# A fused attention and two-layer chain on one core: weight loads issued by ScalarE, a softmax moved to VectorE, weight combinations spread out

## The chip, the cores and the metric

One core of a Trainium2 chip runs the whole program in one launch. The metric is the device time of one execution in microseconds (us), the median of the runs shown. One further execution was profiled, and all rows below are of that one. A difference of about 0.2% (2.7 us) is what repeated runs of this kernel can tell from none.

## What is computed

Chunked attention (batch 8, 8 heads, 576 positions, chunks of 64, head size 64), then two feed-forward stages over the 4608 tokens of width 512:

```python
scores = scale * q_c @ k_c.T                 # per chunk of 64
attn = exp(scores - max) ; attn /= sum + 1e-9
x = (attn @ v_c) as [4608, 512]
h = x @ w_in                                 # [512, 2048]
x = (max(h, 0) + log1p(exp(-abs(h)))) @ w_out
h = max(max(x @ w1, x @ w2), x @ w3)         # [512, 768] each
out = h @ w_out2
```

The weights arrive as 64-bit floats and are turned into pairs of 32-bit parts on VectorE. Every product is done three times, on high and low parts (the table `PASS`), so TensorE runs 128x128 by 128x512 matrix multiplications nearly all the time.

## The kernel before

The 4608 tokens are nine blocks of 512. Blocks 0 to 2 go straight through the first feed-forward stage (`mlp1`). Blocks 3 to 8 go in three pairs by a scheme that saves one product in eight: seven products (`p1` to `p7` of `UnitA`) for each of eight **units** of a pair, where a unit is two columns of weights for both blocks. The weights of a unit are combinations made once (`weightsa`, during block 2), stored in DRAM as `wac` (three to a unit) and `wae` (one to two units), and loaded again for each pair by `againa`: 77 loads of 512 KB in all, each into one of six places named `ringa`. The last stage, `Triple`, works on three blocks at once with combinations `w2c` of its weights, made by `weights3` and stored in DRAM.

Every piece of work is an entry of a `Plan` (class `Plan`): the engines that may do it with a cost for each, what it reads and writes, what places it needs and a due time. `Plan.order` runs through a clock of its own, takes the entry with the earliest due time among those that are ready and whose places are free, and so writes down one fixed order for each engine. On the chip each engine then works through its list in order and waits at a row until what that row needs is there. So a row that waits holds up all rows behind it on its engine, data transfers that the engine issues among them.

Four things of this stage matter here:
- `againa` (L1034 to L1053) puts the loads of a unit's weights on GpSimd's queue, beside the loads of `v` (`loads`, L468), the stores of combinations (`w2c`, L926; `wso`, L1233) and the loads of the later weights (`conv`, L318).
- The attention tiles of blocks 5 to 8 are done between the units (`attention` with `apart=True`). Their `softmax` subtracts the maximum inside eight ScalarE activations, one for each 64 columns, which also accumulate the sums (L562).
- `keep` (L1134) copies a product of a unit out of the PSUM bank `ph`, which the next product into this bank needs back; `soft` (L1143) is the activation, and `cut_up` splits its result into high and low parts `g` for the second matrix. `finish` (L773) copies four accumulator banks `acc` out at the end of a block.
- `combos` (L1203) makes combinations of the second matrix for the last pair. The table `COMBOS` (L986) says behind which step of pair 0's second half each of its four calls stands.

## Time and profile before

| | |
|---|---|
| median of the runs (3 runs, lowest and highest) | 1368.36 us (1367.06, 1369.38) |
| the profiled execution, its own time | 1365.48 us |
| its span, first to last instruction | 1363.6 us |
| granted TensorE clock, mean over the span | 0.994 |
| TensorE busy with matrix multiplications | 1333.2 us, 98% |
| VectorE, ScalarE, GpSimd busy | 983.7, 545.0, 321.7 us |
| bytes moved | 289.38 MB, mean 212 GB/s |

Times in rows count from the first instruction of the span. Block 2 ends and pair 0 begins at about 340 us, pair 1 at about 517, pair 2 at about 679; the last stage begins near 830. Lines such as L1120 are those of the kernel before: L1120 is a product of a unit, L1419 the second matrix, L597 the small products of an attention tile, L281 a copy or cast on ScalarE, L288 a two-operand instruction on VectorE, L1156 the activation, L1045 a load of a unit's weights.

### The profile page before, as it was taken

How to read it: one execution, taken by the hardware profiler on the slowest of the kernel's cores; microseconds unless marked ns; L12 is line 12 of the kernel's file. 1: busy time of each engine (PE TensorE's matmuls, PEld its weight loads, DVE VectorE, ACT ScalarE, POOL GpSimd, SP SyncE). 2: the span in 40 equal slices, each digit the busy share in tenths (PEclk: the TensorE clock that was granted, in tenths of full speed). 3: DMA queues.
4: the chain of work that ended last, by engine and by line, in shares of the span. 5: the costliest groups of instructions: out<-in, count | busy, mean ns of one | idle time of the engine just before them, and what ended most of it. 6: DMA issues, size and time to landing. Idle time of an engine off the chain costs nothing.

```text
span 1363.6 us, 23089 instructions
## 1 busy us (share of the span) xinstructions
PE 1333.2 (98%) x8616; PEld 1094.0 (80%) x8616; DVE 983.7 (72%) x1527; ACT 545.0 (40%) x1199; POOL 321.7 (24%) x561
## 2 busy tenths in 40 slices
PE   5899999999999999999999999999999999999998
PEld 4788887888888887787788887888888888888887
DVE  8999965797576898657868898779714597145951
ACT  4544434464544645445535454432123222132211
POOL 2011555542233324323211122121111122011100
PEclk8999999999999999999999999999999999999999
DMA  8565567677689999978966789655644465344401
GB/s 254 159 201 154 134 181 201 189 273 228 169 257 258 267 302 301 280 252 297 366 209 237 259 311 338 234 192 193 219 162 144 155 231 206 141 148 154 139 25 68
DMA packets 218863, 289.38 MB, mean 212 GB/s; under 512 B 121601, under 2 KB 146625, under 8 KB 218753
## 3 DMA queue, kind: packets, MB, share of 16 engines
q0 software_dynamic: 53792, 178.26, 38.1%
q1 hardware_dynamic: 164144, 108.87, 26.9%
q8 instruction: 68, 1.11, 0.3%
q10 hardware_dynamic: 816, 0.79, 0.2%
q14 instruction: 43, 0.34, 0.1%
HBM read 196.61 MB, written 91.23 MB: 211 GB/s over the span
## 4 chain that ended last, share of the span: by engine, by line
PE 86%; DVE 5%; issue 4%; DMA 2%; POOL 1%; ACT 1%; SPq 0%; DVEq 0%; POOLq 0%; ACTq 0%
PE acc L1567 14%; PE both L1567 13%; PE acc L825 10%; PE ph L805 9%; PE ph L1120 8%; PE acc L1419 7%; PE one L1120 6%; PE both L1665 6%; PE acc L1665 5%; PE acc L1342 2%; PE ph L1342 2%; PE acc L1265 2%; DVE s L288 1%; PE aps L503 1%; POOL rv L468 1%
## 5 line engine op out<-in xcount | busy, mean ns | idle before, releaser
L288 DVE TENSOR_TENSOR s<-s,s 128x1024 f32<-128x1024 f32 (+3 forms) x222 | 213.8, 992 | 11.8 <-DMA x2d<-s 5.5
L1419 PE MATMUL acc<-g,s 128*128 128x512 f32 x768 | 184.5, 393 | 3.0 <-ACT tmp L281 2.2
L1419 PEld LDWEIGHTS acc<-g,s 128*128 128x128 f32 x768 | 142.6, 188 | 35.2 <-ACT tmp L281 3.1
L1120 PE MATMUL ph<-s,s 128*128 128x512 f32 x576 | 144.1, 389 | 1.4 <-DMA s<-wac 0.7
L805 PE MATMUL ph<-s,s 128*128 128x512 f32 x576 | 140.4, 394 | 0.0
L825 PE MATMUL acc<-g,s 128*128 128x512 f32 x576 | 139.8, 392 | 0.0
L1120 PEld LDWEIGHTS ph<-s,s 128*128 128x128 f32 x576 | 108.0, 188 | 24.6 <-DMA s<-wac 1.2
L805 PEld LDWEIGHTS ph<-s,s 128*128 128x128 f32 x576 | 108.3, 189 | 23.1
L825 PEld LDWEIGHTS acc<-g,s 128*128 128x128 f32 x576 | 107.3, 188 | 22.6
L281 ACT CAST s<-s 128x512 fp32r<-128x512 f32 (+1 forms) x106 | 86.3, 831 | 93.4 <-DVE s L1598 31.2
L1567 PE MATMUL acc<-s,s 128*128 128x512 f32 x452 | 120.3, 389 | 0.0
L1550 POOL DMA_DIRECT2D s<-w2c x105 | 56.0, 533 | 266.2 <-PE both L1567 87.5
L281 ACT CAST g<-s 128x1024 fp32r<-128x1024 f32 (+1 forms) x64 | 58.7, 919 | 144.6 <-PE both L1567 37.3
L1567 PE MATMUL acc<-g,s 128*128 128x512 f32 x400 | 110.0, 389 | 0.0
L1120 PE MATMUL one<-s,s 128*128 128x512 f32 x432 | 106.4, 390 | 0.9 <-ACT p L562 0.9
L1567 PE MATMUL both<-s,s 128*128 128x512 f32 x400 | 106.3, 389 | 0.0
L288 DVE TENSOR_TENSOR g<-tmp,g 128x512 fp32r<-128x512 f32 x104 | 70.6, 680 | 44.3 <-ACT g L281 44.2
L1567 PE MATMUL both<-g,s 128*128 128x512 f32 x368 | 100.1, 389 | 0.0
L1567 PEld LDWEIGHTS acc<-s,s 128*128 128x128 f32 x452 | 84.9, 188 | 17.6
L1120 PEld LDWEIGHTS one<-s,s 128*128 128x128 f32 x432 | 80.9, 188 | 18.5 <-ACT p L562 1.8
L468 POOL DMA_DIRECT2D rv<-in_v_dram x103 | 63.5, 620 | 104.5 <-issue 55.3
L1567 PEld LDWEIGHTS both<-s,s 128*128 128x128 f32 x400 | 75.1, 188 | 15.6
(158 smaller groups left out, 2159.5 us busy)
## 6 DMA issues: line engine op xcount, KB each, us to landing
s<-w2c POOLq DMA_DIRECT2D x105, 512.0 KB, 4.5
s<-wac POOLq DMA_DIRECT2D x66, 512.0 KB, 6.5
w2c<-s POOLq DMA_DIRECT2D x45, 512.0 KB, 5.2
wac<-s POOLq DMA_DIRECT2D x24, 512.0 KB, 5.1
s<-in_moe_w_dram POOLq DMA_DIRECT2D x18, 512.0 KB, 5.6
s<-x2d POOLq DMA_DIRECT2D x18, 512.0 KB, 5.8
s<-in_moe_w_in_dram SPq DMA_DIRECT2D x16, 512.0 KB, 6.2
s<-in_moe_w_out_dram SPq DMA_DIRECT2D x16, 512.0 KB, 5.7
```

What stands on the lines that cost most here:

```text
L281: nc.scalar.copy(dst(), src())
L288: return op({"D": 0.69 * n}, lambda e: nc.vector.tensor_tensor(dst(), a(), b(), f), r=r, w=w, **kw)
L468: dma(out=dst().rearrange("p (c e d) -> p c e d", e=2, d=D)[half * CH:(half + 1) * CH, lo:lo + mine, h, :], in_=v[b, t % HP * 2 + h].rearr ...
L805: nc.tensor.matmul(ph.t, w[:, wi, kk * P:(kk + 1) * P], x[kk].t[:, xi], start=(kk == 0 and wi == 0 and xi == 0), stop=(kk == KD - 1 and wi ...
L825: nc.tensor.matmul(acc[m // 2].t[:, m % 2], w[:, wi, m * P:(m + 1) * P], g.t[:, gi, :], start=(first and wi == 0 and gi == 0), stop=(last ...
L1120: nc.tensor.matmul(dst(), ws.t[:, wi, col + kk * P:col + (kk + 1) * P], x[kk].t[:, xi], start=(first and kk == 0 and wi == 0 and xi == 0), ...
L1265: nc.tensor.matmul(u.acc[f].t[:, m], w.t[:, wi, m * P:(m + 1) * P], g.t[:, gi, :], start=(first and wi == 0 and gi == 0), stop=(last and w ...
L1342: nc.tensor.matmul(dst(m), lhs(wi, nn, m), (GH, GL)[gi].t[:, nn], start=(fresh and nn == 0 and wi == 0 and gi == 0), stop=(nn == 1 and wi ...
L1419: nc.tensor.matmul(acc[half].t[:, m % 2], w.t[:, wi, m * P:(m + 1) * P], g.t[:, gi, :], start=(first and wi == 0 and gi == 0), stop=(last ...
L1550: lambda e, k=k, z=z: nc.gpsimd.dma_start(out=z.t.bitcast(F32), in_=w2c[s][late + k]),
L1567: nc.tensor.matmul(bank.view()[:, f], ws(wi, slice(f * HT + kk * P, f * HT + (kk + 1) * P)), (XH, XL)[xi].t[:, kk], start=(first and kk == ...
L1665: nc.tensor.matmul(banks[t // 2].view()[:, t % 2], (GH, GL)[gi].t[:, f, t * P:(t + 1) * P], wo2_of[j].t[:, wi], start=(j == 0 and wi == 0 ...
```

## The change

The loads of `againa` are issued by ScalarE. In the plan a place of `ringa` is handed out again only 2.0 us after it came free (`rest`); the program itself has no such pause. The softmax of tiles between units is done with two subtractions and a sum on VectorE and one activation of 512 columns on ScalarE. The four calls of `combos` stand behind steps 1, 5, 9 and 13 of pair 0's second half, which were 1, 4, 7 and 10.

```diff
--- before.py
+++ after.py
@@ -61,6 +61,7 @@
     def __init__(self, places):
         self.ops = []
         self.free = {k: list(v) for k, v in places.items()}
+        self.rest = {}
 
     def op(self, engs, fn, r=(), w=(), alloc=(), hold=(), after=(), due=None, lat=0.0, move=0.0):
         o = Op()
@@ -118,6 +119,7 @@
         waiting = sorted((o for o in ops if not o.left), key=lambda o: (o.due, o.n))
         running = []
         now, done, moved = 0.0, [], {}
+        resting = []
         while len(done) < len(ops):
             taken = []
             virt = dict(engine)
@@ -161,8 +163,12 @@
                 gone = set(taken)
                 waiting = [o for o in waiting if o not in gone]
             times = [t for t in engine.values() if t > now] + [o.end for o in running] + [o.ready for o in waiting if o.ready > now]
+            times += [t for t, _, _ in resting]
             assert times, "nothing can go on"
             now = min(times)
+            for item in [r for r in resting if r[0] <= now]:
+                resting.remove(item)
+                self.free[item[1]].append(item[2])
             ended = [o for o in running if o.end <= now]
             if ended:
                 running = [o for o in running if o.end > now]
@@ -170,7 +176,10 @@
                     for b in o.bufs:
                         b.uses -= 1
                         if b.uses == 0 and b.place is not None:
-                            self.free[b.place[0]].append(b.place[1])
+                            if b.place[0] in self.rest:
+                                resting.append((now + self.rest[b.place[0]], *b.place))
+                            else:
+                                self.free[b.place[0]].append(b.place[1])
                     for s in o.succ:
                         s.left -= 1
                         s.ready = max(s.ready, o.end + (0.13 if set(s.engs) == {o.eng} else 0.2))
@@ -271,6 +280,7 @@
         pool.tile([P, 2, TB], F32R, tag=f"s{i}", name=f"s{i}_0")
     drop = pool.tile([P, 1], F32, name="drop")
     plan = Plan(places)
+    plan.rest = {"ringa": 2.0}
     op = plan.op
 
     def copy_op(dst, src, r, w, psum=False, n=1.0, engs="DA", **kw):
@@ -745,7 +755,7 @@
         if t >= NTILE:
             return
         pbuf = Buf("p")
-        softmax(None if apart else G, pbuf, True, True)
+        softmax(None if apart else G, pbuf, not apart, not apart)
         PT = slot(*("vh", "z", "w")[:2 + (t > 2 * HP + 3)], dt=F32)
         pt, pT = half(PT, 0), half(PT, 1)
         op({"D": 0.69}, lambda e: nc.vector.transpose(
@@ -983,7 +993,7 @@
     GDLAT = 8.0
     SOON = 4
     SEVENS = (2,)
-    COMBOS = (('out', 0, 1), ('out', 0, 4), ('out', 0, 7), ('out', 0, 10))
+    COMBOS = (('out', 0, 1), ('out', 0, 5), ('out', 0, 9), ('out', 0, 13))
     LATER = (7, 0)
     SLACK = 0.0
     MORE = (3, 0), (5, 0), (5, 0)
@@ -1041,8 +1051,8 @@
         rings_a[:] = ring
         for k in (0, 2, 1, 3)[:len(new)]:
             o = op(
-                {"G": 1.0},
-                lambda e, k=k: nc.gpsimd.dma_start(out=new[k].t.bitcast(F32), in_=wac[n][k] if k < 3 else wae[n // 2]),
+                {"A": 0.5},
+                lambda e, k=k: nc.scalar.dma_start(out=new[k].t.bitcast(F32), in_=wac[n][k] if k < 3 else wae[n // 2]),
                 w=[new[k]],
                 alloc=[ring[k][0], new[k]],
                 after=[store["a", n, k] if k < 3 else store["a", n + 1, k], began[GATE]],
```

The order of TensorE's rows is the same in both kernels; the lists of the other engines are the same up to about the beginning of pair 0. Names in the rows below end in buffer numbers: `s15_325` is a tile in slot 15, and the next tile with `s15` uses the same memory.

**GpSimd's queue near the end of pair 1**: the weights of pair 2's first units (`wac`, `wae`), the loads of one tile's `v` (`rv`), and the first stores of `w2c`. Before:

```order
L894 DMA s41_314_7083<-w2d1_105 128x1024
L1045 DMA s12_319_7151<-wac0_2_157 128x1024
L1045 DMA s10_321_7158<-wac0_1_156 128x1024
L1045 DMA s25_323_7182<-wae0_179 128x1024
L468 DMA rv0_88<-in_v_dram 64x4x64 x4
L926 DMA w2c0_0_183<-s0_320_7153 128x1024
L318 DMA s38_326_7230<-in_moe2_w1_dram 128x4x256
L926 DMA w2c1_0_186<-s5_322_7162 128x1024
L926 DMA w2c2_0_189<-s18_324_7191 128x1024
L926 DMA w2c3_0_192<-s6_325_7228 128x1024
L1045 DMA s30_328_7265<-wac1_0_158 128x1024
L926 DMA w2c4_0_195<-s33_329_7268 128x1024
```

Now:

```order
L904 DMA s43_314_7013<-w2d1_105 128x1024
L328 DMA s35_321_7090<-in_moe2_w1_dram 128x4x256
L478 DMA rv0_88<-in_v_dram 64x4x64 x4
L936 DMA w2c0_0_183<-s5_319_7081 128x1024
L936 DMA w2c1_0_186<-s1_320_7086 128x1024
L936 DMA w2c2_0_189<-s10_322_7120 128x1024
L936 DMA w2c3_0_192<-s12_323_7124 128x1024
L936 DMA w2c4_0_195<-s15_325_7158 128x1024
L936 DMA w2c5_0_198<-s7_328_7195 128x1024
L936 DMA w2c6_0_201<-s10_332_7228 128x1024
```

The five loads of `wac` and `wae` are gone from this queue, and the stores follow directly on the loads of `rv`; a load for `conv` has moved ahead of them.

**ScalarE at the start of pair 1**: `finish` of a block (`tmp` from `acc`), the softmax of a tile (`p`), and `keep` of the unit's first product (a copy from `ph1`). Before:

```order
L281 COPY tmp3_81<-acc1_96 128x512
L281 COPY tmp6_84<-acc0_95 128x512
L281 COPY tmp1_79<-acc0_95 128x512
L562 ACTIVATE p0_89,mx2_72<-one0_4211,mx3_73 128x64 x4
L562 ACTIVATE p0_89,mx2_72<-one1_4212,mx3_73 128x64 x4
L281 COPY tmp0_78<-ph1_93 128x512
L281 CAST s1_271_6171<-s34_263_6016 128x512
L1156 ACTIVATE tmp4_82<-tmp4_82 128x512
L281 CAST s15_273_6187<-tmp8_86 128x512
L1156 ACTIVATE tmp7_85<-ph0_92 128x512
L281 COPY tmp8_86<-ph1_93 128x512
```

Now:

```order
L291 COPY tmp4_82<-acc0_95 128x512
L291 COPY tmp8_86<-acc0_95 128x512
L597 ACTIVATE p0_89<-p0_89,drop_299 128x512
L291 CAST s6_270_6099<-s32_262_5974 128x512
L291 CAST s32_271_6113<-tmp0_78 128x512
L1166 ACTIVATE tmp5_83<-tmp5_83 128x512
L291 COPY tmp0_78<-ph1_93 128x512
L1166 ACTIVATE tmp1_79<-ph0_92 128x512
L1055 DMA s8_274_6153<-wac2_2_163 128x1024
L291 COPY tmp3_81<-ph1_93 128x512
L1166 ACTIVATE tmp2_80<-tmp2_80 128x512
L1166 ACTIVATE tmp0_78<-tmp0_78 128x512
```

The eight activations (two rows of four) have become one row at L597, three rows of casts and an activation (L1166) stand ahead of the first copy from `ph1`, and a load of weights is in the list. The activation ahead of that copy, on `tmp5`, is that of product `p5`.

**ScalarE at the end of pair 1**: the activation of product `p4` (read from `ph1`), the cast of its `g0`, and the four copies out of `acc`. Before:

```order
L1156 ACTIVATE tmp4_82<-ph1_93 128x512
L281 CAST g2_77<-s15_316_7119 128x512
L281 CAST g0_75<-tmp4_82 128x512
L281 CAST s37_327_7263<-s8_266_6076 128x512
L281 CAST s33_329_7268<-s32_313_7082 128x512
L1156 ACTIVATE tmp1_79<-tmp1_79 128x512
L281 CAST s0_330_7279<-s34_278_6272 128x512
L281 COPY tmp6_84<-acc1_96 128x512
L281 COPY tmp3_81<-acc1_96 128x512
L281 CAST g0_75<-s15_316_7119 128x512
L281 COPY tmp7_85<-acc0_95 128x512
L281 COPY tmp8_86<-acc0_95 128x512
```

Now, in two pieces that follow on each other:

```order
L1166 ACTIVATE tmp3_81<-ph1_93 128x512
L291 CAST s36_326_7167<-s29_267_6039 128x512
L291 CAST s5_327_7183<-s32_277_6222 128x512
L291 CAST g0_75<-tmp3_81 128x512
L291 CAST s7_328_7195<-s38_312_7011 128x512
L291 CAST s37_329_7198<-s40_284_6392 128x512
L291 CAST s33_330_7201<-s41_291_6558 128x512
L1055 DMA s1_331_7209<-wac0_1_156 128x1024
L1166 ACTIVATE tmp5_83<-tmp5_83 128x512
L291 COPY tmp4_82<-acc1_96 128x512
L291 COPY tmp0_78<-acc1_96 128x512
```

```order
L291 CAST s10_332_7228<-s22_313_7012 128x512
L291 COPY tmp3_81<-acc0_95 128x512
L291 CAST s12_333_7242<-s38_312_7011 128x512
L291 CAST s39_334_7251<-s8_300_6748 128x512
L291 CAST s18_335_7254<-s27_311_7002 128x512
L1055 DMA s0_336_7257<-wae0_179 128x1024
L1166 ACTIVATE tmp1_79<-tmp1_79 128x512
L1055 DMA s6_337_7268<-wac1_0_158 128x1024
L1055 DMA s15_338_7273<-wac1_2_160 128x1024
L291 CAST s35_339_7291<-s40_284_6392 128x512
L291 COPY tmp5_83<-acc0_95 128x512
```

Before, the cast of `s0_330` and, two rows on, the copies out of `acc1` stand behind the store of `w2c0`, whose source is slot 0. Now the cast of `s5_327`, ahead of the cast of `g0`, uses the slot that the store of `w2c0` reads; the load into `s1_331`, ahead of the first copy out of `acc1`, uses that of `w2c1`; and the load into `s15_338`, ahead of the last copy out of `acc0`, uses that of `w2c4`.

## Rows read from the trace of the kernel before

**Rows 1.** The page: busy time, share of the span and instructions of each engine.

```profile
PE 1333.2 (98%) x8616; PEld 1094.0 (80%) x8616; DVE 983.7 (72%) x1527; ACT 545.0 (40%) x1199; POOL 321.7 (24%) x561
```

**Rows 2.** Who TensorE waited for, 68 us to the end: total us, times, longest.

```profile
PE acc L1419 <- ACT tmp L281: 2.2, 2, 2.0
PE acc L1342 <- ACT s L281: 1.6, 1, 1.6
...
PE one L1120 <- ACT p L562: 0.9, 2, 0.6
PE ph L1120 <- DMA s<-wac: 0.7, 1, 0.7
```

**Rows 3.** Timeline of TensorE and GpSimd, 530 to 554: start, us, engine, line, [idle before].

```profile
542.74 1.66 POOL L468 DMA_DIRECT2D rv<-in_v_dram  x3 [1.27 <-issue]
...
545.42 1.07 POOL L1045 DMA_DIRECT2D s<-wac  x2
...
543.11 2.88 PE L1120 MATMUL one<-s,s 128*128 128x512 f32 x12
...
552.13 1.65 PE L1120 MATMUL ph<-s,s 128*128 128x512 f32 x6 [0.74 <-DMA s<-wac]
```

**Rows 4.** Timeline of ScalarE, 517 to 528, and of TensorE there.

```profile
520.06 0.34 ACT L562 ACTIVATE p<-one,mx 128x64 f32<-128x64 f32 x1
...
522.61 0.59 ACT L281 COPY tmp<-ph 128x512 f32<-128x512 f32 x1
...
525.03 0.63 ACT L1156 ACTIVATE tmp<-tmp 128x512 f32<-128x512 f32 x1 [0.52 <-DVE tmp L288]
...
524.11 2.88 PE L1120 MATMUL ph<-s,s 128*128 128x512 f32 x12
```

**Rows 5.** Timeline of GpSimd at the end of pair 1, 613 to 660.

```profile
627.79 1.11 POOL L1045 DMA_DIRECT2D s<-wac  x2 [4.69 <-PE one L1120]
...
630.48 1.31 POOL L468 DMA_DIRECT2D rv<-in_v_dram  x2 [0.80 <-PE one L597]
635.51 0.63 POOL L468 DMA_DIRECT2D rv<-in_v_dram  x1 [3.73 <-issue]
639.12 0.62 POOL L468 DMA_DIRECT2D rv<-in_v_dram  x1 [2.98 <-PE one L1120]
639.73 0.56 POOL L926 DMA_DIRECT2D w2c<-s  x1
```

**Rows 6.** Timeline of ScalarE, 628 to 646, and of TensorE, 640 to 656.

```profile
637.27 0.62 ACT L281 CAST g<-tmp 128x512 fp32r<-128x512 f32 x1 [1.14 <-issue]
...
643.54 0.62 ACT L281 CAST s<-s 128x512 fp32r<-128x512 f32 x1 [3.27 <-DMA w2c<-s]
644.07 1.06 ACT L281 COPY tmp<-acc 128x512 f32<-128x512 f32 x2
...
645.19 3.06 PE L1419 MATMUL acc<-g,s 128*128 128x512 f32 x12 [1.98 <-ACT tmp L281]
...
648.80 7.55 PE L1419 MATMUL acc<-g,s 128*128 128x512 f32 x32
```

**Rows 7.** By line: issues of transfers, duration ns min/median/max; landing us min/median/max (L1045, L926).

```profile
L1045 POOL DMA_DIRECT2D s<-wac x66: 528/538/771, 316.1 to 764.7; - x66
DMA to landing us min/median/max: 3.5/6.5/11.3
...
L1325 SPq DMA_DIRECT2D s<-wso x16: 319/320/658, 767.1 to 826.9; - x16
L443 SPq DMA_DIRECT2D rq<-in_q_dram x160: 311/447/2241, 68.8 to 557.9; - x160
...
DMA to landing us min/median/max: 2.9/5.2/13.7
```

**Rows 8.** Groups by form, 340 to 690: count, busy us, mean ns, idle before.

```profile
L288 DVE TENSOR_TENSOR tmp<-one,tmp 128x512 f32<-128x512 f32 x48 | 33.0, 687 | 35.4 <-PE one L1120 35.3
L545 DVE TENSOR_REDUCE mx<-one 128x4 f32<-128x256 f32 x28 | 11.4, 414 | 2.6 <-ACT s L281 2.2
```

## The prediction

> **What bounds the kernel now.** The page's first part comes first: TensorE is busy 1333.2 us, 98% of the span [rows 1], and the order of its rows does not change, so the change can only touch its waits. The list of these waits from 68 us on says how much there is to win: four groups of it belong to the stretch that the change rewrites, 2.2, 1.6, 0.9 and 0.7 us, the last two for the softmax activations and for a load of `wac` [rows 2]. Everything in reach is about 5.4 us, 0.4% of the time. Next come the timelines around the longest of them, to see what each is made of.
>
> At 552.13 a unit's first product waited 0.74 us for its weights. On GpSimd three loads of `rv` stand ahead of that load, and it was issued at 545.42, though TensorE had freed its place before 543.11 [rows 3]. At 520.06 ScalarE began the eight activations of a softmax, and `keep` behind them came at 522.61 [rows 4]: 2.55 us of one engine in one piece. The longest, 1.98 us at 645.19, is a chain: TensorE waits for two copies out of `acc` at 644.07, these stand on ScalarE behind a cast at 643.54 that waited 3.27 us for a store of `w2c` [rows 6], and that store left GpSimd only at 639.73, behind four loads of `rv` of which the third and fourth waited 3.73 and 2.98 us [rows 5]. ScalarE's wait is the visible one; GpSimd's full queue is the cause.
>
> **The change part by part.** The sum starts from the profiled execution, 1365.48 us (span 1363.6); the median of the runs shown is 2.88 us above it, and that is added at the end.
>
> *The 77 loads leave GpSimd.* The wait for `wac` goes: in the new list the load stands behind a copy from `ph`, which follows the product that ends before 543.11, so it can leave at about 543.9, 1.5 us earlier, against 0.74 us needed. **-0.74**. Ahead of the `w2c` stores at the end of pair 1 the loads at 627.79 and after it are gone [rows 5]. If the four `rv` issues then follow on each other, 4 x 0.63 us from 630.48, the first store leaves near 633.0 instead of 639.73 and lands, with the median 5.2 us of these stores [rows 7], at 638.2; the second store follows 0.56 us later, and the copies behind them are wanted at 645.19 less 1.98, 643.2 [rows 6]. **-1.98**; the other bound is no gain and a loss, which is a rival below.
>
> Here a page bears on it. The rows show the third `rv` issue resuming at 635.51, some 7.7 us after the first `wac` load left at 627.79 [rows 5], and loads of `wac` take 3.5 to 11.3 us to land [rows 7], so I read the wait as room that has to come free in GpSimd's queue. The Trainium skill (SBUF — State Buffer, the box on "DVE blocks DMA" in "SBUF: two separate sides") puts it otherwise: GpSimd cannot write descriptors while VectorE holds their shared port. By that rule the loads of `rv` would stall as before, beside a busier VectorE, and the sum would lose the 1.98 us of gain. The issues themselves, 528 to 771 ns over 66 loads [rows 7], show no such stretching, so I stay with the first reading.
>
> *77 issues on ScalarE.* No row shows a 512 KB load from there. The nearest are SyncE's issues of loads of this size, 319/320/658 ns; the upper end is SyncE's crowded issues of `q`, up to 2241 [rows 7]. I take 0.32 to 0.45: 25 to 35 us of a ScalarE that is busy 40% [rows 1], spread over 450 us. Hidden behind TensorE where a product or two lie between; where not, the items below count it. A load that waits for its place now holds ScalarE. Its place is one that TensorE freed earlier, and the plan's pause of 2 us mostly keeps the load's row behind work that comes later than that. But the weights are asked for up to 2 us later too. For the load at 552.13 the time from leaving (543.9) to its use (551.4 without the wait) is 7.5 us, against 6.5 us of median landing and 11.3 of the longest [rows 7]; about one such load stands in each unit. I take **+0.5** in all, bounds 0 and 3.
>
> *Softmax of the 14 tiles.* ScalarE: 2.55 us become one activation of 0.63 (the activation of 512 columns at 525.03 [rows 4]), so it gets about 27 us back, as much as the issues cost. The two waits of TensorE on the softmax go: **-0.93** (0.9 in [rows 2]). VectorE: two subtractions of 256 columns, near the reduction of that size, 414 ns, and a sum over 512 columns, near 687 [rows 8], less a small scaling: about 1.4 us each, 20 us in all. It lies beside TensorE; VectorE is busy 72% of the span [rows 1], and its cover is the product or two between a tile's scores and their use two tiles later. I take 0; without that cover each tile would cost at most its 1.4 us.
>
> *What is late next.* At the start of pair 1 `keep` of the first product now stands behind the activation of `p5`. That activation ran from 525.03 for 0.63 us, a copy takes 0.59, so the copy ends at about 526.2; the product that needs the bank started as the second half of the row at 524.11, at about 525.5 [rows 4]. **+0.8**, bounds 0 and 1.5. At the end of pair 1 the cast of `g0`, done at 637.27 before [rows 6], gets two casts ahead of it, the second in the slot that `w2c0` must leave, at 638.2 by the estimate above: **+0.6**, bounds 0 and 1.6. The fourth copy out of `acc` gets eight rows between it and the third, three of them loads: 4 casts and one activation at some 0.55 us and three issues at 0.4, 3.9 us. The bank is wanted at 648.80 less the 1.98 that went [rows 6], 646.8. If the first two copies end at 643.2, when TensorE wants them, the third (0.59), those 3.9 us and the fourth (0.59) end at 648.3; the first two can be some tenths earlier. **+1.0**, bounds 0 and 3.
>
> *`combos` wider apart* moves the same instructions; its last call now falls at the start of pair 1, and the row above has its price. Cost 0 beyond it.
>
> Sum: -0.74 - 1.98 - 0.93 + 0.5 + 0.8 + 0.6 + 1.0 = -0.75. That is 1364.7 for the profiled execution and **1367.6 us** for the median: no change that can be told (about 0.2%, 2.7 us, can).
>
> **The rivals.**
> *A, the forecast*: 1367.6, with its bounds 1365.7 to 1371.0. Chance 0.50.
> *B, the waits go and no new ones come.* The pause of 2 us is only in the plan; on the chip a load leaves as soon as its place is free and its row is reached, and rows that look late in a list cost nothing if their data come later still. Then -0.74 - 1.98 - 0.93 = -3.65 stands alone: 1364.7; with half of the 1.6 us of L1342 [rows 2], which a reshuffled list may lose, 1363.9. For it speaks that GpSimd's queue is the root of the two longest waits that I followed; against it the three places above. Chance 0.25.
> *C, slower: ScalarE is held by a load whose slot a `w2c` store has not left.* At the end of pair 1 the load into `s1_331` needs `w2c1` landed and stands ahead of all four copies out of `acc`. If the `rv` issues still wait as in [rows 5], `w2c1` leaves at 640.3 and lands at 645.5 (5.2 us, up to 13.7 [rows 7]); then one issue, one activation and two copies, 0.4 + 0.63 + 1.06 [rows 6], end at 647.6, 2.4 us later than before instead of 1.98 earlier: +4.4, so 1372.0. It decides from a landing of `w2c1` later than 2.1 us before 643.2, so after about 641. Against it: three of the transfers that filled the queue are gone. Chance 0.17.
> *D, slower: issues on ScalarE take as long as SyncE's worst.* SyncE's issues of `q` reach 2241 ns against a median of 447 [rows 7]. At 1.2 us an issue, between the two, the three loads ahead of the fourth copy add 2.4 us and the short leads 1.5: 1371.5. The Trainium skill (Perfetto Trace Analysis, "DMA Instruction — HWDGE") has such a cause, one descriptor generator that the issuing engines lock in turn; no row of this trace has two such engines issuing at once. Chance 0.08.
>
> **How the numbers follow.** Faster by over 0.2%: B, 0.25. Within: A, 0.50. Slower: C and D, 0.25. The range runs from 1363.6, just below B, to 1372.4, just above C.
>
> **What would show it.** The waits of TensorE on `wac` and on the softmax are gone from the list; the issues of L1055 on ScalarE last 0.3 to 0.5 us; the first store of `w2c` leaves within 3 us of the first of the four `rv` loads ahead of it. Wrong would be a wait of TensorE of over 2 us behind copies out of `acc` near 645 (C), a median of these issues near 1 us (D), or a list without waits at 525 and 645 (B).

## The result: 0.9% slower, and the profile after

The changed kernel takes 1379.64 us (median of six runs, 1378.87 to 1389.38) against 1369.78 of the kernel before (six runs): a ratio of 1.0089, 95% interval 1.0060 to 1.0118, over all runs (the two medians alone give 1.0072; one run of 1389.38 lies far above the rest). I had forecast no change, 1367.6, with a range up to 1372.4 and a chance of 0.25 for slower. The profiled execution took 1379.49 us with a span of 1377.6, 14.0 us more than that of the profiled execution before. The count below is of these two executions.

The page of the changed kernel, busy time by engine (before: [rows 1]):

```profile
PE 1335.7 (97%) x8616; PEld 1094.8 (79%) x8616; DVE 994.2 (72%) x1552; ACT 523.7 (38%) x992; POOL 277.9 (20%) x484
```

TensorE issues the same 8616 products; ScalarE and GpSimd both have less to do. The loss is in waits and, as the rows show, in the slow products behind two of them. Who TensorE waited for, from 68 us on (before: [rows 2]):

```profile
PE acc L1429 <- ACT g L291: 5.6, 1, 5.6
PE acc L1429 <- ACT tmp L291: 5.5, 1, 5.5
PE ph L1130 <- ACT tmp L291: 2.1, 2, 1.4
PE one L1130 <- DVE tmp L298: 1.4, 1, 1.4
PE aps L513 <- DMA s<-pd: 1.3, 2, 1.1
PE acc L1352 <- ACT s L291: 1.2, 1, 1.2
```

The waits on `wac` and on the softmax are gone, as forecast, and so is the one of 1.98 us. Two new waits of 5.5 us stand at the ends of pair 0 and pair 1, and behind each TensorE runs at half its clock for a while. Granted clock (PEclk, the third figure from the end) and busy time, by windows of the changed kernel:

```profile
464.00:470.00 6.00, 5.85 (x43) 4.24 (x44) 5.28 (x11) 2.42 (x5) 0.00 (x0) 1.00 0.59 183
...
476.00:479.00 3.00, 2.60 (x6) 2.12 (x7) 2.23 (x4) 1.52 (x4) 1.06 (x2) 0.50 1.05 390
...
650.00:656.00 6.00, 5.52 (x12) 4.10 (x13) 4.10 (x8) 4.11 (x8) 0.53 (x1) 0.50 1.01 348
656.00:660.00 4.00, 4.00 (x17) 3.21 (x16) 3.60 (x7) 2.78 (x5) 0.04 (x1) 0.89 1.08 389
```

The count closes. End of pair 0: 5.54 us of waiting and 1.4 of slow products (19 products take 5.95 us below; at the pace of 32 in 7.55 us in [rows 6] they take 4.5); end of pair 1: 5.55 and 3.2 (12 products take 5.79 us below, 3.06 in [rows 6], and the clock of 0.89 over the next 4 us costs another 0.4); 1.38 at 446 us and 1.40 at 532: 18.5 in all. Gone are 2.2, 0.9 and 0.7 us [rows 2], 0.3 of the 1.6 of L1342, and 0.8 of smaller waits: 4.9. That makes 13.6 of the 14.0 us.

**The end of pair 0 and SyncE.** The loads themselves went as priced. The issues of line 1055 in the changed kernel (duration min/median/max; then issue to landing):

```profile
L1055 ACTq DMA_DIRECT2D s<-wac x66: 326/327/956, 315.9 to 780.9; - x66
...
DMA to landing us min/median/max: 3.1/5.5/9.1
```

What they did to another queue, I had not priced. What SyncE waited for from 300 to 700 us in the changed kernel, the three largest of its rows for `wac` and `wae`, which make 31.3 us in all (no such row exists before):

```profile
SPq L453 <- DMA s<-wac: 16.2, 10, 4.6
...
SPq L879 <- DMA s<-wac: 5.0, 3, 2.4
SPq L1172 <- DMA s<-wac: 4.9, 4, 2.4
```

SyncE's loads of `q` and `k` (`rq` and `rk` in the rows; `gd`, `pd` and `x2d` are buffers in DRAM that are stored to and loaded from again) need nothing from `wac`. But each transfer names a semaphore on which its landing is counted, and in these records SyncE and ScalarE take eight of them (100 to 107) in turn, GpSimd eight others. An issue waits until the last transfer with its semaphore has landed: of the 1200 issues of the changed kernel for which the records tell that landing, none starts before it. Drawn from the records of the changed kernel (not a view of the profile):

```
issued  queue    transfer  semaphore  landed
432.57  ScalarE  wac       103        437.15
437.17  SyncE    rq        103        442.48
448.15  SyncE    rq        105        453.57
453.63  SyncE    gd        105        459.06
```

So 77 loads with a median of 5.5 us to landing now share SyncE's turns, and SyncE runs late. The timelines of ScalarE, SyncE, VectorE and TensorE show what came of the wait at 437:

```profile
432.57 0.33 ACTq L1055 DMA_DIRECT2D s<-wac  x1
...
437.17 1.35 SPq L453 DMA_DIRECT2D rq<-in_q_dram  x3
...
443.40 0.71 DVE L708 STREAM_TRANSPOSE s<-rq 128x512 f32<-128x512 f32 x1 [4.67 <-DMA rk<-in_k_dram]
...
448.03 1.21 PE L1130 MATMUL one<-s,s 128*128 128x512 f32 x4 [1.38 <-DVE tmp L298]
```

The load of `q` left when `wac` had landed, VectorE's transpose stood still for it, and with VectorE the sum that TensorE needed at 446.6. (The transpose's row names `rk`, but by the records no load of `rk` lands before 444.15, and the last of `rq` lands at 443.18.) At 470 the same lateness does more. ScalarE, SyncE and TensorE there:

```profile
463.01 0.63 ACT L1166 ACTIVATE tmp<-tmp 128x512 f32<-128x512 f32 x1
...
475.76 0.59 ACT L291 COPY tmp<-acc 128x512 f32<-128x512 f32 x1 [6.91 <-DMA gd<-tmp]
...
469.05 0.38 SPq L1172 DMA_DIRECT2D gd<-tmp  x1
...
476.40 5.95 PE L1429 MATMUL acc<-g,s 128*128 128x512 f32 x19 [5.54 <-ACT tmp L291]
```

The activation at 463.01 fills a `tmp` buffer whose store to `gd` could leave at 463.7. It left at 469.05, behind `rk`, `pd` and `gd` transfers that ran late on SyncE, and landed at 475.7. The fourth copy out of `acc` needs that buffer.

**The end of pair 1.** GpSimd, ScalarE and TensorE in the changed kernel (before: [rows 5, 6]):

```profile
636.38 0.77 POOL L328 DMA_DIRECT2D s<-in_moe_w_dram  x1 [7.61 <-PE ph L1130]
637.14 1.05 POOL L478 DMA_DIRECT2D rv<-in_v_dram  x1
644.50 1.85 POOL L478 DMA_DIRECT2D rv<-in_v_dram  x3 [6.32 <-PE acc L1429]
646.34 2.77 POOL L936 DMA_DIRECT2D w2c<-s  x5
...
649.29 0.62 ACT L291 CAST s<-s 128x512 fp32r<-128x512 f32 x1 [7.15 <-DMA w2c<-s]
649.81 0.61 ACT L291 CAST g<-tmp 128x512 fp32r<-128x512 f32 x1
...
635.85 0.69 PE L607 MATMUL one<-s,rv 64*64 64x64 f32 x32
...
650.48 5.79 PE L1429 MATMUL acc<-g,s 128*128 128x512 f32 x12 [5.55 <-ACT g L291]
```

TensorE's rows keep their order, so times can be counted from one of its rows, the product with `rv` (629.37 before, 635.85 now). From there the first store of `w2c` leaves after 10.36 us before [rows 5] and after 10.49 now: the queue that lost its loads is no faster. What changed is the row behind the store: the cast of `g0`, which TensorE wants after 9.1 us, now stands behind the cast that waits for the store. Before, it stood ahead of it [rows 6].

Why GpSimd is no faster: the profile puts the 6.32 us on TensorE, but the records say room. They tell into how many pieces each transfer is cut: a load of `rv` 256, `in_moe_w` 512, `wac` and `w2c` 128. In each of these stalls the load leaves 0.32 to 0.33 us after the landing that brings the pieces underway, its own included, under 1024. Now: 512 + 256, and the next 256 wait for `in_moe_w` (landed 644.17, left 644.50). Before: the third load of [rows 5] left at 635.51 behind a `wac` that landed at 635.19, the fourth at 639.12 behind an `rv` that landed at 638.79.

### The profile page after: what moved, and what is told of

The parts are those of the page before. It is cut to its first block, busy times and chain, and to the rows that moved or that the text cites. A ratio compares the mean times of both kernels' runs of the same rounds, so it can differ in the third digit from the quotient of the medians.

```text
span 1377.6 us, 22845 instructions
## 1 busy us (share of the span) xinstructions
PE 1335.7 (97%) x8616; PEld 1094.8 (79%) x8616; DVE 994.2 (72%) x1552; ACT 523.7 (38%) x992; POOL 277.9 (20%) x484
## 4 chain that ended last, share of the span: by engine, by line
PE 84%; DVE 7%; DMA 4%; issue 3%; SPq 1%; ACT 1%; POOL 1%; DVEq 0%; POOLq 0%; ACTq 0%
PE acc L1577 14%; PE both L1577 12%; PE acc L835 9%; PE ph L815 9%; PE acc L1429 9%; PE ph L1130 9%; PE one L1130 6%; PE both L1675 6%; PE acc L1675 5%; DVE s L298 3%; PE acc L1275 1%; PE aps L513 1%; DVE tmp L298 1%; PE one L607 1%; DMA rk<-in_k_dram 1%
## 5 line engine op out<-in xcount | busy, mean ns | idle before, releaser
L1429 PE MATMUL acc<-g,s 128*128 128x512 f32 x768 | 189.1, 399 | 11.3 <-ACT g L291 5.6
L835 PE MATMUL acc<-g,s 128*128 128x512 f32 x576 | 139.8, 392 | 0.0
L1577 PE MATMUL acc<-g,s 128*128 128x512 f32 x400 | 110.0, 389 | 0.0
L298 DVE TENSOR_TENSOR tmp<-one,tmp 128x512 f32<-128x512 f32 x72 | 49.6, 689 | 56.5 <-PE one L1130 56.0
```

The lines of the kernel that those rows point to most:

```text
L298: return op({"D": 0.69 * n}, lambda e: nc.vector.tensor_tensor(dst(), a(), b(), f), r=r, w=w, **kw)
L835: nc.tensor.matmul(acc[m // 2].t[:, m % 2], w[:, wi, m * P:(m + 1) * P], g.t[:, gi, :], start=(first and wi == 0 and gi == 0), stop=(last ...
L1429: nc.tensor.matmul(acc[half].t[:, m % 2], w.t[:, wi, m * P:(m + 1) * P], g.t[:, gi, :], start=(first and wi == 0 and gi == 0), stop=(last ...
L1577: nc.tensor.matmul(bank.view()[:, f], ws(wi, slice(f * HT + kk * P, f * HT + (kk + 1) * P)), (XH, XL)[xi].t[:, kk], start=(first and kk == ...
```

## The experiments

Eighteen kernels, with four to ten runs each. A ratio is to runs of the kernel before that were taken beside it. Waits are TensorE's, in us, in two stretches of the profiled execution (400 to 520, end of pair 0; 620 to 680, end of pair 1); SyncE's are those for landings of `wac` and `wae`, 300 to 700.

| kernel | ratio to before [95%] | pair 0 | pair 1 | SyncE |
|---|---|---|---|---|
| before | 1 | 0.7 | 2.3 | 0 |
| the change | 1.0089 [1.0060, 1.0118] | 6.9 | 5.6 | 31.3 |
| b1 only the issue | 1.0151 [1.0114, 1.0188] | 9.1 | 6.7 | 36.0 |
| b2 all but the issue | 1.0011 [0.9993, 1.0029] | 0.0 | 3.2 | 0 |
| b3 all but combos | 1.0087 [1.0063, 1.0110] | 7.4 | 6.3 | 33.2 |
| b4 all but softmax | 1.0152 [1.0130, 1.0174] | 7.8 | 7.4 | 40.7 |
| y1 old order, ScalarE issues | 1.0032 [1.0011, 1.0052] | 1.6 | 3.5 | 47.3 |
| x1 new order, GpSimd issues | 1.0054 [1.0036, 1.0071] | 1.6 | 7.2 | 0 |
| x2 new order, SyncE issues | 1.0104 [1.0073, 1.0136] | 7.5 | 6.4 | 35.6 |
| f3 | 1.0086 [1.0052, 1.0121] | 5.6 | 6.4 | 39.5 |
| f1 | 1.0079 [1.0055, 1.0103] | 8.0 | 7.7 | 33.5 |
| f5 | 1.0108 [1.0090, 1.0125] | 6.6 | 7.7 | 38.1 |
| f7 | 1.0081 [1.0052, 1.0110] | 8.3 | 5.8 | 42.3 |
| f2 | 1.0097 [1.0073, 1.0121] | 8.0 | 8.7 | 42.2 |
| f6 | 1.0075 [1.0060, 1.0089] | 3.6 | 7.6 | 33.3 |
| f8 | 1.0078 [1.0048, 1.0108] | 2.2 | 6.8 | 32.4 |
| f9 | 1.0073 [1.0040, 1.0106] | 8.5 | 5.9 | 33.5 |
| f10 | 1.0088 [1.0058, 1.0118] | 2.4 | 8.9 | 37.1 |
| g1 | 1.0046 [1.0031, 1.0060] | 0.0 | 9.0 | 0 |
| g2 | 1.0011 [0.9997, 1.0025] | 0.0 | 5.4 | 0 |

### One part of the change at a time

b1 keeps only the first part (the queue and the pause), b2 leaves only it out. The edit of b2 in the changed kernel, shortened:

```diff
-    plan.rest = {"ringa": 2.0}
+    plan.rest = {}
...
-                {"A": 0.5},
-                lambda e, k=k: nc.scalar.dma_start(...
+                {"G": 1.0},
+                lambda e, k=k: nc.gpsimd.dma_start(...
```

b3 takes `COMBOS` back to 0, 1, 4, 7, 10, and b4 takes the softmax back to `softmax(None if apart else G, pbuf, True, True)`; b1 does both.

> The kernel before with one part of the change alone: ScalarE issues the 77 loads, with the pause of 2 us in the plan. Theory Q (queues): in the trace of the change every transfer of SyncE and ScalarE counts its landing on one of eight semaphores taken in turn by both queues (100 to 107), so a load of wac that takes 5 to 7 us to land holds SyncE's eighth issue after it, and SyncE runs late. Then SyncE waits at least 15 us in all for landings of wac (before: none), and the time is 1373 to 1380 us. Theory V (VectorE): the softmax on VectorE makes VectorE's results late, and the issue is free; then this kernel takes 1367 to 1371. Theory K (the distance of the combos): also 1367 to 1371.

> The change without its first part: GpSimd issues the 77 loads as before and there is no pause, softmax on VectorE and combos at 0, 1, 5, 9, 13 of the change stay. Q: SyncE waits for no landing of wac, TensorE has no wait of over 2.5 us between 440 and 660 us, and the time is 1366 to 1371 us. V or K: a wait of 5 us or more at the end of a pair stays, and the time is 1374 to 1380.

> The change with the combos left where they were before (0, 1, 4, 7, 10). Q: at least one wait of TensorE of over 4 us at the end of a pair stays, since the loads still share SyncE's semaphores: 1373 to 1380 us. V: the same, 1374 to 1380. K: both long waits go, 1364 to 1371.

> The change with the softmax of the 14 tiles left on ScalarE. Q: at least one wait of TensorE of over 4 us at the end of a pair stays: 1373 to 1381 us. V: both long waits go and the time is 1366 to 1371. K: 1374 to 1380.

Q holds against V and K: all three kernels that issue from ScalarE lose 0.9 to 1.5% and have SyncE's waits, the one that doesn't loses nothing that can be told. Its numbers were not all right: b1 and b4, at 1386.63 and 1387.70 us, are slower than its 1380 and 1381, and b2 has a wait of 3.03 us where it gave at most 2.5. V falls, and more: with ScalarE issuing, the kernel with the softmax on VectorE loses 0.9% and the one without it 1.5 (the change and b4), and with GpSimd issuing, VectorE's softmax costs nothing that can be told (b2). The distance of the combos does nothing (b3). These kernels are each put in an order of their own, so the queue and the order are still mixed, in the difference between b4 and the change too.

### The queue apart from the order

Here each instruction keeps its place in the program, and the 77 loads change their queue alone:

```diff
-                lambda e, k=k: nc.scalar.dma_start(...
+                lambda e, k=k: nc.gpsimd.dma_start(...
```

x1 is this, x2 the same with `nc.sync`, y1 the reverse edit in the kernel before.

> The changed kernel with every instruction in the changed order, but the 77 loads leave from GpSimd's queue at the same places of the program. Theory Q: SyncE waits for no landing of wac, its stores of gd leave on time, and the wait of 5.54 us at 470 is gone; GpSimd's own queue gets its old waits for room back, so a wait near 645 stays: 1368 to 1376 us. Rival H (ScalarE is held or disturbed by the changed order of its own rows, softmax and combos): the wait at 470 stays above 4 us and the time is 1376 or more.

> The changed kernel with every instruction in the changed order, but the 77 loads leave from SyncE at the same places of the program. Theory Q: they still take every turn of the same eight semaphores, so SyncE still waits at least 15 us in all for landings of wac, and has 77 issues of 0.33 us or more in addition; the wait at 470 stays above 4 us and the time is 1376 or more. Rival H: the harm comes from ScalarE, which is held at its issues and lets SyncE wait for loads that it has not issued yet; then the waits shrink and the time is 1366 to 1372.

> The kernel before with every instruction in its old order (no pause, softmax and combos as before), but the 77 loads leave from ScalarE at the same places of the program. Theory Q: the queue alone does it: SyncE waits at least 10 us in all for landings of wac, ScalarE is held at its issues, a wait of TensorE of over 3 us appears, 1373 us or more. Rival H: the harm of the change is in its new order and not in the queue: 1366 to 1371.

TensorE's waits from 400 to 520 in x1, where the change has 5.5 and 1.4:

```profile
PE acc L1429 <- ACT tmp L291: 1.6, 1, 1.6
```

What SyncE waited for in y1, 300 to 700, second row of the list:

```profile
SPq L443 <- DMA s<-wac: 22.6, 10, 4.7
```

Q is shown for SyncE's waits: they are there in every kernel whose loads take those semaphores, SyncE's own loads in x2 included, and in no other. (The Trainium skill, "DMA: Bandwidth & Descriptors", section "Issuing engines are not separate DMA queues", says that another issuing engine saves only the sequencer's time; here even less came of it.) But the queue alone is not the whole: old order and ScalarE 0.32% slower, new order and GpSimd 0.54%, both together 0.89%. They nearly add up, though the intervals are wide. Two more pairs show what an order costs. y1 and b1 both issue from ScalarE and do the same work; b1 has the order that the plan made for this, and loses 1.51% where y1 loses 0.32. x1 and b2 both issue from GpSimd; x1 has the order made for ScalarE's issues, and loses 0.54% where b2 loses 0.11. So most of b1's loss comes with its order; in the old order the queue's own price is y1's.

Two forecasts of Q missed. y1 is at 1371.47 us instead of 1373 or more, and its longest wait of TensorE is 2.3 us, not over 3: with 47 us of SyncE's waits it has 1.6 us of TensorE's at pair 0, so that order leaves SyncE more slack. In x2 the wait at 470 is gone, and TensorE waits 7.22 us at 437 to 444 for a load of `wac` itself, which stands in SyncE's late list. x1, at 1376.95, is also 1 us above Q's range.

### The end of pair 0

f3 sends the one store of 469.05 from GpSimd (operation 2136 in the order of their making):

```diff
+        for n in (2136,):
+            plan.ops[n].eng = "G"
```

> The changed kernel with its order kept, but one store changes its queue: the store of a tmp buffer to gd at 469.05 us (activation of p5 at 463.01) leaves from GpSimd, which is idle from 460.4 to 470.7, instead of SyncE. Theory Q: the store was ready at 463.7 and stood 5.4 us behind SyncE's late loads; from GpSimd it leaves near 463.8 and lands near 470, the fourth copy out of acc gets its tmp buffer at 470.4, and TensorE's wait of 5.54 us at 470.8 falls under 1 us with the 1.4 us of half clock behind it: 1371.5 to 1374 us. Rival: the landing is slow because the DMA engines are full, whatever the queue; then the wait falls by less than 2 us and the time is 1377 to 1380.

The store left at 463.94 and the copy came at 470.77, 5 us earlier, as theory Q has it; the wait of 5.54 us at 470 is gone. But the time, 1380.90 us, did not come down: SyncE's next late transfer took its place. TensorE's waits from 400 to 520 in f3:

```profile
PE one L607 <- DMA s<-pd: 3.6, 2, 2.8
PE acc L1429 <- ACT tmp L291: 1.0, 1, 1.0
PE one L1130 <- DVE tmp L298: 1.0, 1, 1.0
```

### The end of pair 1

The order is changed by hand, after the plan is made:

```diff
-        for o in plan.order():
+        plan.order()
+        for n, behind in ((2896, 3489),):
+            plan.ops[n].start = plan.ops[behind].start + 0.01
+        for o in sorted(plan.ops, key=lambda o: (o.start, o.n)):
```

This is f1: the load of `in_moe_w` (2896) behind the first store of `w2c` (3489). In f5 the four loads of `rv` and then this load go behind the second store, in f7 the four loads alone, in f2 nothing on GpSimd, but on ScalarE the waiting cast (2970) behind the cast of `g0` (2935).

> The changed kernel with its order kept, but one load moved on GpSimd: the load of in_moe_w at 636.38 us, in 512 pieces of 1 KB, goes behind the four loads of rv and the first store of w2c instead of ahead of them. Theory R (room): GpSimd's queue holds a limited number of pieces, fewer than 1024 underway at once in every stall of both traces (conv 512 + rv 256 go, the next 256 wait until conv has landed at 644.17 and leave at 644.50), so without the 512 pieces the four rv loads follow on each other, the first w2c store leaves near 639.6 instead of 646.34, the cast behind it is not held, and TensorE's wait of 5.55 us near 645 shrinks to under 1.5 us, with the stretch at half clock behind it (3.2 us): 1371 to 1374 us. Rival: the profile puts the 6.32 us of the rv load down to TensorE (acc L1429); if that is so, the loads still leave at 644.5 and the time stays at 1378 to 1381.

> The changed kernel with its order kept, but on GpSimd at the end of pair 1 the first two stores of w2c go ahead of the four loads of rv and the load of in_moe_w that stood in front of them. Theory R: these loads hold GpSimd for room (1024 pieces are never underway at once: 512 + 256 go and the next 256 wait in the changed kernel, 3 x 256 go and the fourth waits in the run with the load of in_moe_w moved); ahead of them the first store of w2c leaves near 637.3 us instead of 646.34, lands by 643, the casts follow, and TensorE's wait of 5.55 us near 645 falls under 1 us, with the 3.2 us of half clock behind it: 1370 to 1374 us. Rival: the store itself lands late because the DMA engines are full there, and TensorE still waits over 3 us: 1376 to 1381.

> The changed kernel with its order kept, but only the four loads of rv at the end of pair 1 go behind the first two stores of w2c; the load of in_moe_w stays in front. Theory R (order and room on GpSimd): 512 + 128 + 128 pieces fit under 1024, so w2c leaves near 637.2 and 637.8 us and lands by 644.5, in_moe_w lands near 644 as before, TensorE's wait near 645 is under 1 us and no wait of VectorE for in_moe_w follows: 1369 to 1374 us. Rival (the DMA engines are full there whatever the order): a wait of over 4 us stands somewhere between 640 and 670, 1377 to 1382.

> The changed kernel with its order kept, but on ScalarE the cast of g0 goes ahead of the cast into the slot that the first store of w2c must leave (649.29 us), as it stood before the change. Theory S (the row behind the waiting one): the cast of g0 runs near 642, TensorE has its 24 products with g0 in hand while the store lands, the wait of 5.55 us at 645 and the 3.2 us of half clock go, and the copies out of acc, now behind the waiting cast, cost about 2 us as before the change: 1371.5 to 1375 us. Rival T (transport): as with the reordered loads, the wait only moves to the copies out of acc and TensorE waits 4 us or more in all between 640 and 670: 1376 to 1381.

GpSimd in f1:

```profile
638.99 2.15 POOL L478 DMA_DIRECT2D rv<-in_v_dram  x3 [7.81 <-PE one L607]
646.86 0.62 POOL L478 DMA_DIRECT2D rv<-in_v_dram  x1 [5.71 <-issue]
647.47 0.56 POOL L936 DMA_DIRECT2D w2c<-s  x1
```

Theory R holds and my number fell: three loads of `rv` go, the fourth waits until the first has landed (646.53), for four of them are 1024 pieces by themselves. In f5 the stores go first, and the wait of 5.55 us shrinks to 0.6. TensorE's waits there, 628 to 680:

```profile
PE acc L1429 <- DVE g L293: 6.5, 1, 6.5
PE acc L1429 <- DVE g L298: 0.6, 2, 0.4
PE acc L1429 <- ACT g L291: 0.6, 1, 0.6
```

The 6.5 us are new: VectorE waits for `in_moe_w`, which now leaves last. With it first (f7) the first store lands 9 us after its issue, and the waits are 2.7 and 2.7. With the casts swapped (f2) the cast of `g0` runs at 646.06 without a wait for the store, and TensorE waits for the copies out of `acc` instead:

```profile
PE acc L1429 <- ACT tmp L291: 7.9, 2, 5.0
PE acc L1429 <- DVE g L298: 0.8, 1, 0.8
```

The wait of 5.0 us is that for the fourth copy. SyncE, ScalarE and TensorE there:

```profile
654.51 0.32 SPq L1172 DMA_DIRECT2D gd<-tmp  x1
...
662.63 0.33 ACTq L1055 DMA_DIRECT2D s<-wac  x1
663.00 0.62 ACT L291 CAST s<-s 128x512 fp32r<-128x512 f32 x1 [4.46 <-DVE s L293]
663.52 0.58 ACT L291 COPY tmp<-acc 128x512 f32<-128x512 f32 x1
...
664.15 8.18 PE L1429 MATMUL acc<-g,s 128*128 128x512 f32 x27 [5.03 <-ACT tmp L291]
```

The profile puts ScalarE's 4.46 us on VectorE, but the records say semaphore: the load of `wac` at 662.63 takes semaphore 105, which the store of `gd` at 654.51 had taken before it, and that store landed at 662.55. The load's place was free at 658.08 (the store of `w2c4` had landed) and the row ahead of it was done at 658.53, so some 4 us of the wait are the shared turn. It is theory Q from the other side: ScalarE waits for a transfer of SyncE, and its copies stand behind. The same load is held by a store of `gd` in f10 (4.1 us, wait of 4.98) and in f1 (3.0 us, wait of 2.93).

So each move cures what it aims at, and 5.6 to 8.9 us of waits stay between 620 and 680 in every kernel that has the change's order. The times are those of the rivals to within 0.5 us (1381.06, 1380.93, 1378.71 and 1381.44), 4.7 to 7.1 us above the most that R and S gave; their cause, DMA engines that are full in any order, is shown only in part. For it speaks that in f5 the first store took 7.1 us to land, against a median of 5.2 [rows 7]; against it that f7 has no wait of over 4 us there, and that the longer wait in f2 and f10 is mostly a semaphore's.

### Both ends, and tries at a faster kernel

f6, f8, f9 and f10 are to cure pair 0 by f3's move, with five loads of `rk` behind four of `pd` on SyncE. At pair 1, f6 is f5, f8 is f7, f10 is f2, and f9 sends two stores of `w2c`, then `in_moe_w`, then `rv`. g1 and g2 start from b2, with the moves of f5 and f7, and four transposes behind the softmax's subtractions on VectorE.

> The run before this one, and at the end of pair 0 the store of gd from GpSimd as in the run with that one move, with the five loads of rk on SyncE put behind the four loads of pd that TensorE waited for there. Theory Q: SyncE is late as a whole behind the landings of wac, so taking two of its transfers out of the way removes the waits of 5.54 us at 470 and 5.55 us at 645, and what is left are the smaller waits: 1364 to 1370 us. Rival: SyncE's lateness reaches TensorE through the next transfer in line (rk, x2d or gd) and a new wait of over 2.5 us stands between 460 and 500: 1371 to 1377.

> The run before this one with the two moves at the end of pair 0 (the store of gd from GpSimd, the five loads of rk behind the loads of pd). Q and R: neither of the two long waits is left; what stays are the 2.2 us near 493 and the 1.8 near 531 of the earlier run with these moves: 1365 to 1370 us. Rival: as above, 1375 to 1380.

> The changed kernel with its order kept, but at the end of pair 1 GpSimd takes first the two stores of w2c, then the load of in_moe_w, then the four loads of rv; and the two moves at the end of pair 0 (the store of gd from GpSimd, five loads of rk behind four loads of pd on SyncE). Theory R (order): w2c leaves at 637.3 and 638 and lands by 645, in_moe_w leaves near 639 and lands by 647, before VectorE asks for it near 650; TensorE has no wait of over 1 us between 640 and 670, and with the moves at pair 0 the time is 1364 to 1370 us. Rival T (transport): the transfers of that stretch take too long in any order, a wait of over 3 us stays between 640 and 670, 1373 to 1380 us.

> The run before this one with the two moves at the end of pair 0 (the store of gd from GpSimd, five loads of rk behind four loads of pd on SyncE). S and Q: neither long wait is left, 1366 to 1371 us, within 0.2% of the kernel before. Rival: SyncE's lateness and the full DMA engines give new waits of over 3 us: 1374 to 1380.

> A try for a kernel that beats both: the change without ScalarE's issues (GpSimd issues the 77 loads), with the stores of w2c ahead of the loads of rv as above, and the transposes of rq and rk of two tiles behind the two subtractions of the softmax on VectorE that free TensorE's banks (VectorE waited 5.04 us for rk at 585.5 with these behind it). Theories R and Q: the two longest waits of that kernel, 3.03 us at 643 and 2.14 at 586, go with the half clock behind each (1.4 us each): about 8 us from 1368.1, 1360 to 1364 us, 0.3 to 0.5% under the kernel before. Rival: the waits move on by one row, and it stays within 1365 to 1369.

> The change without ScalarE's issues, with only the four loads of rv behind the first two stores of w2c (the load of in_moe_w and two loads of wac stay in front) and the four transposes moved as before. R: the wait of 3.03 us at 643 and the 8.7 us that the earlier try made there are gone: 1361 to 1366 us, 0.2 to 0.4% under the kernel before. Rival: a wait of over 3 us stays between 635 and 660: 1367 to 1372.

None of these came out as Q, R or S had it. f8, f10 and g2 lie where their rivals put them; f6, f9 and g1, at 1378.01, 1381.38 and 1372.59 us, are slower than even the rivals allowed. In f8 and f10 the waits of pair 0 fall to 2.2 and 2.4 us, and the time hardly moves: the intervals of all four overlap that of the change. In f9 SyncE's lateness came back at another row (4.6 us at 448, no edit near it), and in f1 and f7 that same wait, 1.38 us in the change, was 2.7 and 2.4. No kernel of these beats the one before; b2 and g2 cannot be told from it. g1 is slower: its order makes TensorE wait 8.7 us at the end of pair 1.

## Why the prediction was wrong, step by step

- **The wait for `wac`, -0.74, and the softmax, -0.93:** right, both are gone, and VectorE's share and the `combos`, taken as 0, show no cost (b2, b3). Beside the new issues the softmax's move is worth more than 0.93, 0.6% between b4 and the change, but their orders differ too.
- **77 issues on ScalarE, +0.5:** the issue costs 327 ns, as taken (0.32 to 0.45). The step failed in what it left out: I counted the time on ScalarE and the way to landing, and never asked what else a transfer holds. It holds a turn of SyncE's semaphores, and takes its own turn behind SyncE's transfers (f2). Measured: 31 us of SyncE's waits, 1.38 us of TensorE's at 446, 5.54 and 1.4 of slow products at 470; in the old order 0.32% of the time (y1).
- **The stores of `w2c`, -1.98:** this is the step that broke the sum. "If the four `rv` issues then follow on each other" could not be: with the load of `in_moe_w` now in front only one goes, and without it only three (f1). My reading of GpSimd's wait as room was right, but I did not look for its size, which [rows 5] held: both loads left 0.3 us after a landing. The page's rule that I weighed there (the Trainium skill, "SBUF — State Buffer", the box on "DVE blocks DMA") gets no support here: landings alone give the end of each of these waits to 0.3 us. No row here shows when VectorE held the shared port, so the rule itself is not tested.
- **The cast of `g0`, +0.6, bounds 0 and 1.6:** mis-sized through the step above, as it took the store's landing from there. Measured 5.55 and 3.2 of slow products.
- **`keep`, +0.8, bounds 0 and 1.5:** measured 1.40 at 532.
- **The fourth copy out of `acc`, +1.0, bounds 0 and 3:** in the changed kernel it is hidden at pair 1 by the wait ahead of it; with that taken away, 5.0 (f2). I had counted the rows ahead of the copy; what held was the turn of a semaphore under one of them.
- **Rivals:** C had the right place and the right cause, a late store of `w2c`, but the wrong store and row (`w2c1` and a load on ScalarE, where `w2c0` and a cast held) and 4.4 us where 8.7 came; I gave it 0.17. D is out: the issues last 327 ns, though 32 of the 77 overlap one of SyncE's. (The trace of before did have two engines issuing at once: at 0.77, 1.28 and 1.83 us ScalarE's three issues overlap SyncE's and last 0.48 to 0.52 us.) Slower than my range needed both ends of pairs; I had looked at one.

Of the 0.89%, by the middle values of the ratios, the new order alone makes 0.54 (x1) and the queue most of the rest. So the terms for the new order (`keep`, the cast, the fourth copy, +2.4 together) were too small as well: x1 loses some 7 us without the queue. Counted from TensorE's rows, the first two stores land no later than before, and yet no order that I tried removes the waits at pair 1. That is only partly explained: by the cast ahead of `g0` (in x1, too, 6.21 us go to it) and by the semaphore ahead of the fourth copy (f2, f10, f1; in x1, whose loads are on GpSimd, that copy costs 0.28). How full the DMA engines are does not tell the two kernels apart: their share is 0.95 to 1.06 there (0.66 from 645 to 650, while TensorE waits), and 0.82 to 1.04 before. What else in the new order makes that stretch too tight stays open.

## What to carry to other kernels

A transfer that changes its queue takes with it whatever that queue's transfers share: look in the trace which semaphore each issue waits for, on both queues that share it, and what stands behind it in line, before pricing the issue's own time. An order that a plan makes for one change is a change of its own: run it with the old queue, and the old order with the new. Count what a queue has underway, in pieces, against what it had when it last stood still. Where an order leaves no slack, curing one wait shows the next, so price the row behind the one that waits.

## What the hardware showed that I had not expected

I had priced a wait by its own length. But TensorE also came back slower: its granted clock was 1.00 up to 470, and 0.50 (the 1.2 GHz level of two, 1.2 and 2.4) from 476 to 479, behind a wait of 5.54 us, and again from 650 to 656, behind 5.55. By the records of single products these then start 427 ns apart instead of 227. Behind the 1.98 us of the kernel before the clock stayed at 1.00 (third figure from the end):

```profile
645.20:648.00 2.80, 2.80 (x12) 2.16 (x12) 2.40 (x5) 2.80 (x6) 1.03 (x2) 1.00 1.00 402
```

In b2 the clock was 0.50 for a while behind a wait of 2.14 us, and again behind one of 3.03, with some six products 427 ns apart each time. The two waits of 5.5 us cost 6.9 and 8.7 us in all.
